# Strided q and k loaded as 108 rows, q/k weights loaded expert by expert, the last output tile in halves, and a new written-out order

## The chip, the cores and the metric

The kernel runs on one core of a Trainium2 chip. The metric is device time in microseconds (us), from one launch. Five engines each work through their own list of instructions in order: PE (TensorE, matrix products and transposes; its weight loads are shown as PEld), DVE (VectorE), ACT (ScalarE), POOL (GpSimd) and SP (SyncE, which here only issues DMA transfers). They wait for one another through semaphores.

## The reference

Inputs: q, k, v of shape (8 batches, 8 heads, 576 tokens, 64), and for each of 4 experts wq, wk, wv (512 x 64) and wo (64 x 512), plus a gate (512 x 4). First an attention with two kinds of sparse heads, then four dense causal attentions over its result, mixed by a top-2 gate:

```python
pos = np.arange(S); rel = pos[:, None] - pos[None, :]
mask_local = (rel >= 0) & (rel < 32)
mask_strided = (rel >= 0) & (pos[None, :] % 32 == pos[:, None] % 32)
# heads 0 to 3 local, heads 4 to 7 strided
x = softmax(where(mask, q @ k.T / 8, -1e9)) @ v      # to (8, 576, 512)
logits = x @ w_gate                                  # two largest of 4 experts, softmax over them
for e in range(4):
    a = softmax(causal((x @ wq[e]) @ (x @ wk[e]).T / 8))
    out += gate_weight(e) * (a @ (x @ wv[e]) @ wo[e])
```

A strided head attends among tokens whose positions agree modulo 32. With 576 tokens that is 32 groups of 18 tokens each.

## The kernel before, in words

**Stage 1** (`stage1(b, hp)`, head pair `hp` of batch `b`) computes the sparse attention of two heads: pairs 0 and 1 are local, 2 and 3 strided. q and k arrive in natural layout in a tile `nat`, are turned so that the 64 channels lie on partitions (tile `qkt`), scores go to PSUM (tiles `bank`), are masked into `p1l` (local) or `p1s` (strided), run through a softmax (maxima and sums on DVE, subtraction and scaling on POOL, the exponential on ACT), are turned back and multiplied with v (tile `v`); the result is written as two parts, `xh` and `xl`, whose sum is the value.

Batches 0 and 1 of the strided pairs turn q and k on PE (the loop at L595 to L609; from batch 2 on, `quad`, DVE does it). There the three residues of a strip of 11 groups lie in one tile: 54 rows of q on partitions 0 to 53, 54 rows of k on partitions 64 to 117, both heads side by side in the columns. Six DMAs bring q and k of such a head pair (L506, three strips each). Each transpose at L603 takes 54 rows by 128 columns, 24 of them per head pair; q's and k's alternate, and lie in different halves of the array's rows.

**Stage 2** (`project`, `values2`, `attend`, `out_tile`) projects x for two experts at a time (`ep` 0: experts 0 and 1; `ep` 1: experts 2 and 3), each product in three parts (L913, L925, L860), does the causal attention (L971, L1008, L1070, L1109) and the output product (L1138), copies the result from PSUM to a tile `ys` and stores it (L1147 to L1150). `load_weights` brings the q and k weights in four blocks of 128 input channels, all four experts in each block, and splits them into a rounded part (`wh`, ACT) and a rest (`wl`, DVE or POOL).

**The order.** The kernel's functions only record operations (`op`). `schedule()` issues them in the order of a table `ORDER`; a set `SECOND` says which operations take the second of two possible engines, and `FILL` says before which operations PE gets that many 128-column products of the identity with itself, whose result nobody reads (L304). So every engine's order follows from these tables. At the very start PE also gets five such products of ones (L1158).

PE's operations come in several tilings of its array (`mode`: "128x128" uses all rows and columns, "64x128" two halves of the rows, "64x64" quarters, and so on).

Of the kernel before, what the change touches and what calls it, by code (L numbers as in the profile page):

```python
# [8 lines left out]
F32 = mybir.dt.float32  # L9
# [11 lines left out]
def attention_moe_kernel(  # L21
# [59 lines left out]
    class Ring:  # L81
# [34 lines left out]
    }  # L116
    ORDER = [
# [1103 lines left out]
```

## Time and profile before

| | us |
|---|---|
| median of 3 runs (lowest to highest) | 440.24 (439.61 to 442.13) |
| the profiled execution, its own time | 439.54 |
| its span, first to last instruction | 437.8 |
| PE busy in it | 428.4 |
| DVE busy | 356.3 |
| ACT busy | 268.3 |
| POOL busy | 231.1 |

The profiled execution's time is 1.7 us more than its span and 0.7 us less than the median of the runs. PE's busy time counts the products that nobody reads too.

### The profile page before, as it was taken

Reading aid. Unit: us, or ns where it says so; the run is one execution under the profiler, and the core shown is the slowest. Engines: PE = TensorE matmul, PEld = TensorE weight load, DVE = VectorE, ACT = ScalarE, POOL = GpSimd, SP = SyncE. Lnnn points to the kernel's source line nnn. Section 1 sums busy time; section 2 is a strip of 40 time slices with the busy share of each in tenths; the row PEclk is TensorE's granted clock in tenths of the full one; section 3 lists DMA queues with packets and bytes.
Section 4 is the critical chain, followed back from the end, with each engine's and each line's share of the span. In section 5 each row is a group of like instructions: output and inputs, shape, how many; then the busy total and the mean of one; then the engine's idle time right before and its main releaser. Section 6 shows DMA issues by size and latency. Waiting matters only on the chain.

```text
span 437.8 us, 18842 instructions
## 1 busy us (share of the span) xinstructions
PE 428.4 (98%) x7588; PEld 376.6 (86%) x7588; DVE 356.3 (81%) x1140; ACT 268.3 (61%) x852; POOL 231.1 (53%) x375
## 2 busy tenths in 40 slices
PE   7999999999999999999999999999999999999996
PEld 6998998997789889788889788998789988998675
DVE  4798999899998896998889888896888888458750
ACT  4486647857676475566665378725577377557743
POOL 4164782678717842843819633679026771417720
PEclk9999999999999999999999999999999999999999
DMA  7665754766635634653256236355241030011113
GB/s 193 155 147 145 144 113 97 148 105 109 125 61 96 122 98 79 137 115 81 51 106 122 76 90 137 73 104 111 73 118 40 1 108 1 26 24 53 70 53 120
DMA packets 156271, 41.87 MB, mean 96 GB/s; under 512 B 145976, under 2 KB 149432, under 8 KB 156184
## 3 DMA queue, kind: packets, MB, share of 16 engines
q1 hardware_dynamic: 156184, 40.67, 42.0%
q8 instruction: 60, 0.98, 0.9%
q14 instruction: 27, 0.22, 0.2%
HBM read 31.20 MB, written 9.44 MB: 93 GB/s over the span
## 4 chain that ended last, share of the span: by engine, by line
PE 86%; DVE 5%; ACT 4%; DMA 2%; issue 1%; SPq 1%; POOL 1%; DVEq 0%; POOLq 0%; ACTq 0%
PE bank L913 19%; PE bank L1138 11%; PE bank L860 10%; PE bank L1109 10%; PE bank L1070 6%; PE bank L971 6%; PE bank L743 3%; PE bank L762 3%; PE bank L304 2%; PE bank L633 2%; PE bank L1008 2%; PE bank L649 2%; PE bank L713 2%; PE bank L925 2%; PE bank L823 1%
## 5 line engine op out<-in xcount | busy, mean ns | idle before, releaser
L1043 POOL TENSOR_SCALAR p<-p,st,wt 128x384 f32<-128x384 f32 (+3 forms) x128 | 77.3, 622 | 42.0 <-DVE st L1034 22.9
L983 ACT ACTIVATE p<-p,st 128x256 f32<-128x256 f32 (+3 forms) x128 | 72.1, 568 | 9.1 <-DVE st L978 8.9
L978 DVE CUSTOM_DVE_ANT_0 p<-bank,m_cau 128x128 f32<-128x128 f32 (+3 forms) x128 | 57.5, 481 | 3.1 <-PE bank L971 2.9
L526 DVE STREAM_TRANSPOSE qkt<-nat 128x576 f32<-128x576 f32 x48 | 47.7, 1004 | 3.5 <-DMA nat<-in_k_dram 3.1
L1109 PE MATMUL bank<-th,vs 128*64 128x192 f32 (+4 forms) x512 | 49.2, 338 | 0.0
L341 ACT COPY th<-bank 128x256 f32<-128x256 f32 (+2 forms) x104 | 40.6, 431 | 12.2 <-PE bank L1070 11.7
L676 POOL TENSOR_TENSOR p1l<-p1l,st 128x640 f32<-128x640 f32 (+1 forms) x18 | 20.7, 1154 | 49.6 <-DVE st L674 40.0
L1109 PEld LDWEIGHTS bank<-th,vs 128*64 128x64 f32 x512 | 34.1, 137 | 14.2 <-issue 7.0
L934 ACT CAST qk<-bank 128x288 fp32r<-128x288 f32 x64 | 25.0, 399 | 30.6 <-PE bank L913 22.8
L725 ACT CAST xh<-bank 128x160 fp32r<-128x160 f32 (+4 forms) x112 | 28.9, 321 | 22.4 <-PE bank L743 9.9
L727 DVE TENSOR_TENSOR xl<-bank,xh 128x160 fp32r<-128x160 f32 (+4 forms) x112 | 31.6, 323 | 6.4 <-ACT xh L725 5.7
L860 PE MATMUL bank<-wh_v,xh 128*128 128x260 f32 x128 | 36.5, 285 | 0.3 <-DVE qkl L936 0.3
L913 PE MATMUL bank<-xh,wh_k 128*128 128x288 f32 x120 | 36.5, 304 | 0.2 <-DVE st L978 0.2
L860 PE MATMUL bank<-wh_v,xl 128*128 128x260 f32 x128 | 36.2, 283 | 0.0
L913 PE MATMUL bank<-xh,wh_q 128*128 128x288 f32 x120 | 36.2, 302 | 0.0
L860 PE MATMUL bank<-wl_v,xh 128*128 128x260 f32 x128 | 36.1, 282 | 0.0
L1070 PEld LDWEIGHTS bank<-ident,p 64*128 64x128 f32 x800 | 30.5, 139 | 6.5 <-issue 3.0
L1070 PE MATMUL bank<-ident,p 64*128 64x64 f32 x800 | 35.2, 227 | 0.5 <-DVE pt L341 0.5
L913 PE MATMUL bank<-xl,wh_q 128*128 128x288 f32 x120 | 35.4, 295 | 0.0
L913 PE MATMUL bank<-xl,wh_k 128*128 128x288 f32 x120 | 35.4, 295 | 0.0
L913 PE MATMUL bank<-xh,wl_k 128*128 128x288 f32 x120 | 35.3, 294 | 0.0
L913 PE MATMUL bank<-xh,wl_q 128*128 128x288 f32 x120 | 35.3, 294 | 0.0
(188 smaller groups left out, 1268.0 us busy)
## 6 DMA issues: line engine op xcount, KB each, us to landing
out_dram<-ys SPq DMA_DIRECT2D x32, 256.0 KB
nat<-in_q_dram SPq DMA_DIRECT2D x96, 72.0 KB
nat<-in_k_dram SPq DMA_DIRECT2D x96, 72.0 KB
v<-in_v_dram SPq DMA_DIRECT2D x96, 40.0 KB
v<-in_v_dram SPq DMA_DIRECT2D x48, 54.0 KB
v<-in_v_dram SPq DMA_DIRECT2D x32, 48.0 KB
v<-in_v_dram SPq DMA_DIRECT2D x32, 45.0 KB
out_dram<-ys SPq DMA_DIRECT2D x8, 128.0 KB
```

Of the source, the lines that this page charges most:

```text
L341: (nc.scalar.copy if e == "ACT" else nc.vector.tensor_copy)(dst, src)
L526: op("tq", {"DVE": 0.66 if local else 1.11}, k0 - 13, lambda e, x=x: nc.vector.transpose(turned(qkt.t, x), raw(x) if local else raw(x).rea ...
L725: op("xh", {"ACT": act(n_) + 0.04 * (not local)}, key, lambda e, s_=s_, x_=x_: nc.scalar.copy(x_(xh.t), s_(xa.t)), r=[xa], w=[xh[u]])
L727: op("xl", {"DVE": dve(n_)}, key + 0.5, lambda e, s_=s_, x_=x_: nc.vector.tensor_sub(x_(xl.t), s_(xa.t), x_(f(xh.t))), r=[xa, xh[u]], w=[x ...
L860: nc.tensor.matmul(vp.t[:, :NV], xx.t[:, t0:t0 + 128], ww.t[:, kt, :], start=i == 0, stop=i == 11)
L913: nc.tensor.matmul(pj.t[:, :HS], ww.t[:, kt, ep * 128:(ep + 1) * 128], xx.t[:, c], start=i == 0, stop=i == 11)
L978: lambda e, sp=sp, p=p, a=a, nk=nk, ci=ci, st=st[ep]: nc.vector.tensor_tensor_reduce(out=p.t[:, a, :nk], in0=sp[a].t[:, :nk], in1=m_cau[:, ...
L983: op("exp2", {"ACT": 0.285 + 0.00084 * nk}, k_ + 1, lambda e, p=p, a=a, ci=ci, nk=nk, st=st[ep]: nc.scalar.activation(p.t[:, a, :nk], p.t[ ...
L1043: lambda e, p=p, a=a, ci=ci, t=t, nk=nk, s_=s_, ep=ep: nc.gpsimd.tensor_scalar(p.t[:, a, :nk], p.t[:, a, :nk], s_.t[:, 20 + ci + a:21 + ci ...
L1070: nc.tensor.transpose(tp[hf].t[:, 64 * c:64 * c + 64], src, ident[r, r])
L1109: nc.tensor.matmul(acc.t[o, c0:c0 + cn], vw, th[ep, a].t[:, s0:s0 + cn], start=j == 0, stop=j == nj - 1, skip_group_check=True)
L1138: nc.tensor.matmul(yp.t[:, :DM], xx.t[:, c0:c0 + 128], ww.t[:, ep, :], start=i == 0, stop=i == 5)
```

## The change

Seven things change. The recorded operations are partly others, so the tables `ORDER`, `SECOND` and `FILL` are new throughout.

1. Strided q and k of batches 0 and 1: one DMA each for q and for k of a head pair, 108 rows (2 heads x 18 x 3 strips) of 11 x 64 elements, instead of three DMAs of 18 partitions and two pieces each. A third strip then has an eleventh group too, which is the next row's first and is masked or not used.
2. The transposes of these take 108 rows by 128 columns, 12 per head pair instead of 24, in the full-array tiling.
3. The order of tokens in a group of 54 is another (position, then strip), so these scores get a mask of their own, `m_tri`, made at the start; v of these pairs is loaded in the same order.
4. wq and wk are loaded and split expert by expert; projections of experts 0 and 1 wait for the weights of these two only.
5. Batch 7's tile 3, the last one stored, is computed, copied and stored in two halves of 256 columns.
6. `FILL` holds 36 products in place of 61.
7. The new `ORDER` and `SECOND`.

```diff
-        8: 5, 13: 6, 18: 7, 51: 1, 56: 3, 76: 1, 89: 4, 92: 5, 96: 1, 124: 4, 131: 2, 148: 4, 208: 2, 218: 1,
-        241: 2, 246: 8, 279: 2, 282: 3, 1132: 2, 1150: 3, 1151: 4,
+        3: 1, 13: 2, 51: 3, 61: 4, 76: 1, 93: 4, 95: 4, 126: 1, 130: 2, 135: 4, 217: 1, 245: 2, 260: 1, 285: 4,
+        292: 2, 1146: 3, 1151: 1, 1157: 8, 1158: 2, 1160: 3,
...
+    m_tri = const.tile([128, 54], F32, name="m_tri")
+    m_res = const.tile([128, 3, NJ + 1], F32, name="m_res")
+    nc.vector.memset(m_res, NEG)
+    for hf in range(2):
+        v_ = m_res[64 * hf:64 * hf + 64, :, :NJ]
+        nc.gpsimd.affine_select(out=v_, in_=v_, pattern=[[-1, 3], [-3, NJ]], compare_op=ALU.not_equal,
+                                fill=0.0, base=0, channel_multiplier=1)
+    nc.vector.tensor_reduce(m_res[:, :, NJ], m_res[:, :, :NJ], axis=mybir.AxisListType.X, op=ALU.max)
+    nc.vector.tensor_copy(m_tri.rearrange("p (u r) -> p u r", r=3), m_res[:, :, NJ].unsqueeze(1).to_broadcast([128, NJ, 3]))
+    for hf in range(2):
+        keep(m_tri[64 * hf:64 * hf + 64], [[-1, 54]], 0, 1)
...
+        if name in "qk":
+            for ex in range(E):
...
+                op("load_0", {"SP": 0.5}, k_ + 0.1 * ex, lambda e, ex=ex, raw=raw: nc.sync.dma_start(
+                    raw(), src[ex].rearrange("(a p) d -> p a d", p=128)), w=[st], dmas=[(0.47, 0.71)])
...
-                for r in range(3):
-                    n_ = (11 if r < 2 else 10) * D
-                    p_ = 64 * x + NJ * r
-                    nc.sync.dma_start(nat.t[p_:p_ + NJ, :22 * D].rearrange("p (h c) -> p h c", h=2)[:, :, :n_], strips(base, 11 * r, n_))
+                nc.sync.dma_start(nat.t[:6 * NJ, 12 * D * x:12 * D * x + 11 * D], triples(base, 0, 2 * NJ, 11))
...
+        def triples(base, g0, m, gn):
+
+            return bass.AP(tensor=base.tensor, offset=base.offset + g0 * D, ap=[[STR * D, m], [11 * D, 3], [1, gn * D]])
...
-                for g in range(6):
-                    for x in range(2):
-                        r = slice(64 * x, 64 * x + 54)
-                        c = (11 * u + 2 * g) * D
-                        nc.tensor.transpose(tp[x].t[:, 54 * g:54 * g + 54], nat.t[r, c:c + 128], ident[r, r])
+                    r = slice(0, 6 * NJ)
+                    for g in range(3):
+                        c = (12 * x + 6 * u + 2 * g) * D
+                        nc.tensor.transpose(tp.t[:, 108 * g:108 * g + 108], nat.t[r, c:c + 128], ident[r, r])
...
     def wbufs(nm, ep=0):
-        return [W[nm][i][kt, ep] for i in range(2) for kt in range({"o": E * D // 128}.get(nm, KT))]
+        parts = range(2 * ep, 2 * ep + 2) if nm in "qk" else range(E * D // 128 if nm == "o" else KT)
+        return [W[nm][i][x] for i in range(2) for x in parts]
...
+        cut = 2 if b == B - 1 and t == 3 else 1
+        n_ = DM // cut
+        for h in range(cut):
...
+                        nc.tensor.matmul(yp.t[:, :n_], xx.t[:, c0:c0 + 128], ww.t[:, ep, c], start=i == 0, stop=i == 5)
...
+                    nc.sync.dma_start(out[b, t0:t0 + 128, c], ys.t[:, c])
```

Where the new tables move instructions, three places show it. The first is SP's list at the start of the program, before the change: `p` and `nat` are the tiles for q and k of stage 1, and a name in brackets is the semaphore waited for; DMAHW0 to DMAHW7 are those of earlier transfers in turn.

```order
L501 DMA p_169<-in_q_dram 128x576
L501 DMA p_169<-in_k_dram 128x576
L501 DMA p_170<-in_q_dram 128x576
L501 DMA p_170<-in_k_dram 128x576
L506 DMA nat_179<-in_q_dram 18x2x704 [waits DVE_49]
L506 DMA nat_179<-in_q_dram 18x2x640
L506 DMA nat_179<-in_k_dram 18x2x704 [waits DMAHW0_49]
L506 DMA nat_179<-in_k_dram 18x2x640 [waits DMAHW1_49]
L501 DMA nat_183<-in_k_dram 128x576 [waits DMAHW2_49,DVE_49]
L427 DMA p_167<-in_moe_w_gate_dram 128x2x4 [waits DMAHW3_49]
L501 DMA nat_183<-in_q_dram 128x576 [waits DMAHW4_49]
```

The same place of SP's list after the change:

```order
L528 DMA p_182<-in_k_dram 128x576
L528 DMA p_182<-in_q_dram 128x576
L530 DMA nat_192<-in_k_dram 108x1x704
L528 DMA p_183<-in_k_dram 128x576
L528 DMA p_183<-in_q_dram 128x576
L530 DMA nat_192<-in_q_dram 108x1x704
L438 DMA p_180<-in_moe_w_gate_dram 128x2x4
L530 DMA nat_195<-in_k_dram 108x1x704
L580 DMA v_205<-in_v_dram 32x5x64 [waits DMAHW0_49]
```

The first strided pair's k stood in the eighth to tenth place and stands in the third; its q stood in the fifth to seventh and stands in the sixth; all of q and k of batch 0's four head pairs but one q is issued before the first transfer that has to wait for an earlier one.

The second place is PE's list behind the five products of ones, before the change: L304 are the products nobody reads, L574 and L587 transposes of local pairs, L603 those of strided pairs, L633 local scores (the alternating rows of one score operation are cut to two).

```order
L304 MATMUL bank1_65<-ident_83 128x128 x5
L574 MATMUL bank1_65<-ident_83,p230_169 128x128 x4
L574 MATMUL bank2_66<-ident_83,p230_169 128x128 x4
L304 MATMUL bank3_67<-ident_83 128x128 x6
L587 MATMUL bank3_67<-ident_83,p230_169 128x128 x2
L574 MATMUL bank4_68<-ident_83,p231_170 128x128 x4
L304 MATMUL bank5_69<-ident_83 128x128 x7
L633 MATMUL bank5_69<-qkt0_191 32x64
L633 MATMUL bank6_70<-qkt0_191 32x64
```

The same place after the change; L305 are the products nobody reads, L608 and L621 the local transposes, L637 the strided ones.

```order
L305 MATMUL bank1_65<-ident_83 128x128
L608 MATMUL bank1_65<-ident_83,p230_182 128x128 x4
L608 MATMUL bank2_66<-ident_83,p230_182 128x128 x4
L305 MATMUL bank3_67<-ident_83 128x128 x2
L621 MATMUL bank3_67<-ident_83,p230_182 128x128 x2
L305 MATMUL bank4_68<-ident_83 128x128 x4
L637 MATMUL bank4_68<-ident_83,nat0_192 128x108 x3
L305 MATMUL bank5_69<-ident_83 128x128 x4
L637 MATMUL bank5_69<-ident_83,nat0_192 128x108 x3
L665 MATMUL bank6_70<-qkt0_201 32x64
L665 MATMUL bank7_71<-qkt0_201 32x64
```

Ahead of the first local scores there stood 18 unread products and stand 11; six strided transposes now come before these scores.

The third place is the end of PE's list, the last output tile, after the change (before it there were six rows of 128x512 into one bank).

```order
L1176 MATMUL bank7_71<-wh_o0_280,oh2_266 128x256
L1176 MATMUL bank7_71<-wh_o0_280,ol2_269 128x256
L1176 MATMUL bank7_71<-wl_o0_281,oh2_266 128x256
L1176 MATMUL bank7_71<-wh_o0_280,oh0_264 128x256
L1176 MATMUL bank7_71<-wh_o0_280,ol0_267 128x256
L1176 MATMUL bank7_71<-wl_o0_281,oh0_264 128x256
L1176 MATMUL bank6_70<-wh_o0_280,oh2_266 128x256
L1176 MATMUL bank6_70<-wh_o0_280,ol2_269 128x256
L1176 MATMUL bank6_70<-wl_o0_281,oh2_266 128x256
L1176 MATMUL bank6_70<-wh_o0_280,oh0_264 128x256
L1176 MATMUL bank6_70<-wh_o0_280,ol0_267 128x256
L1176 MATMUL bank6_70<-wl_o0_281,oh0_264 128x256
```

The first half's six products go to bank 7, the second half's six to bank 6; the copy of bank 7 stands on DVE, that of bank 6 on ACT.

Counted over PE's whole list, changes from one tiling of the array to another fall from 197 to 183.

## Rows read from the trace of the kernel before

**Rows 1.** The page: PE's busy time, and the chain by engine.
```profile
PE 428.4 (98%) x7588; PEld 376.6 (86%) x7588; DVE 356.3 (81%) x1140; ACT 268.3 (61%) x852; POOL 231.1 (53%) x375
PE 86%; DVE 5%; ACT 4%; DMA 2%; issue 1%; SPq 1%; POOL 1%; DVEq 0%; POOLq 0%; ACTq 0%
```

**Rows 2.** Waits of PE, 42 to 438 us: total us, times, longest us.
```profile
PE bank L762 <- issue: 0.8, 1, 0.8
...
PE bank L1008 <- POOL p L996: 0.2, 1, 0.2
```

**Rows 3.** Timeline of PE, the start: start us, us, instruction, shape, count.
```profile
7.00 1.77 PE L304 MATMUL bank<-ident 128*128 128x128 f32 x10
8.61 1.04 PE L574 MATMUL bank<-ident,p 128*128 128x128 f32 x8
9.48 1.50 PE L304 MATMUL bank<-ident 128*128 128x128 f32 x12
10.82 0.38 PE L587 MATMUL bank<-ident,p 128*128 128x128 f32 x2
...
16.89 0.58 PE L603 MATMUL bank<-ident,nat 54*128 54x54 f32 x12
17.41 1.16 PE L304 MATMUL bank<-ident 128*128 128x128 f32 x8
...
22.77 0.95 PE L603 MATMUL bank<-ident,nat 54*128 54x54 f32 x24
23.65 0.71 PE L304 MATMUL bank<-ident 128*128 128x128 f32 x4
...
27.00 1.11 PE L743 MATMUL bank<-pt,v 32*64 32x32 f32 x84
...
42.38 0.40 PE L925 MATMUL bank<-xh,wh_k 128*128 128x288 f32 x1
```

**Rows 4.** Timeline of PE behind a change of tiling.
```profile
45.11 0.40 PE L925 MATMUL bank<-xh,wh_k 128*128 128x288 f32 x1
45.35 0.30 PE L925 MATMUL bank<-xl,wh_k 128*128 128x288 f32 x1
45.48 0.29 PE L925 MATMUL bank<-xh,wl_k 128*128 128x288 f32 x1
```

**Rows 5.** Timeline of SP's DMA issues, the start.
```profile
4.00 1.06 SPq L506 DMA_DIRECT2D nat<-in_k_dram  x3
6.24 0.36 SPq L501 DMA_DIRECT2D nat<-in_k_dram  x1
...
12.46 1.42 SPq L506 DMA_DIRECT2D nat<-in_k_dram  x3
```

**Rows 6.** Timelines of DVE and POOL, their first work on loaded data; idle before in brackets.
```profile
9.75 1.19 DVE L341 COPY qkt<-bank 64x256 f32<-64x256 f32 x3 [4.37 <-PE bank L574]
...
16.04 1.41 POOL L676 TENSOR_TENSOR p1l<-p1l,st 128x320 f32<-128x320 f32 x2 [9.56 <-ACT qkt L341]
```

**Rows 7.** Windows of DVE: stretch, us, busy (count), granted TensorE clock, DMA share, GB/s.
```profile
0.00:20.00 20.00, 11.50 (x63) 1.00 0.65 166
20.00:120.00 100.00, 94.25 (x279) 1.00 0.63 128
120.00:438.00 318.00, 250.57 (x801) 1.00 0.36 81
```

**Rows 8.** Timeline of the end, all engines.
```profile
433.68 0.39 PE L1138 MATMUL bank<-wl_o,oh 128*128 128x512 f32 x1
...
434.11 0.59 ACT L341 COPY ys<-bank 128x512 f32<-128x512 f32 x1 [0.73 <-PE bank L1138]
434.72 0.44 SPq L1150 DMA_DIRECT2D out_dram<-ys  x1
```

**Rows 9.** Groups by line and shape: ACT's copies of 256 columns (busy, mean ns | idle).
```profile
L341 ACT COPY th<-bank 128x256 f32<-128x256 f32 x44 | 15.8, 378 | 5.7 <-PE bank L1070 5.5
```

More of the change, by code (lines that the diff above doesn't have):

```diff
@@ L418, in load_weights @@
         hi, lo = W[name]
-        eps = (0, 1) if name in "qk" else (0,)
         k_ = first("w" + name)
@@ L430, in load_weights, with raw @@
                w=[wide[i][0], wide[i][1]], dmas=[(0.5, 0.2)])
+        if name in "qk":
+            for ex in range(E):
+                st = wide[ex // 2][ex % 2]
+                def raw(ex=ex):
+                    return flat(ex // 2)[:, ex % 2 * n:ex % 2 * n + n].rearrange("p (a d) -> p a d", d=D)
+                c = slice(ex * D, ex * D + D)
+                op("load_0", {"SP": 0.5}, k_ + 0.1 * ex, lambda e, ex=ex, raw=raw: nc.sync.dma_start(
+                    raw(), src[ex].rearrange("(a p) d -> p a d", p=128)), w=[st], dmas=[(0.47, 0.71)])
+                op("hi_w", {"ACT": 0.1 + act(n)}, 15 + k_ * 0.1, lambda e, c=c, raw=raw: nc.scalar.copy(hi.t[:, :, c], raw()),
+                   r=[st], w=[hi[ex]])
+                op("lo_w", {"DVE": 0.1 + dve(n), "POOL": 0.1 + 0.0025 * n}, 15.5 + k_ * 0.1, lambda e, c=c, raw=raw: (
+                    nc.vector if e == "DVE" else nc.gpsimd).tensor_sub(lo.t[:, :, c], raw(), f(hi.t[:, :, c])),
+                   r=[st, hi[ex]], w=[lo[ex]])
+            return
         for kt in range(nk):
@@ L445, in load_weights @@
             op("hi_w", {"ACT": 0.1 + act(n)}, 15 + k_ * 0.1, lambda e, kt=kt, raw=raw: nc.scalar.copy(hi.t[:, kt, :], raw()),
-               r=[st], w=[hi[kt, ep] for ep in eps])
+               r=[st], w=[hi[kt]])
             op("lo_w", {"DVE": 0.1 + dve(n), "POOL": 0.1 + 0.0025 * n}, 15.5 + k_ * 0.1, lambda e, kt=kt, raw=raw: (
                 nc.vector if e == "DVE" else nc.gpsimd).tensor_sub(lo.t[:, kt, :], raw(), f(hi.t[:, kt, :])),
-               r=[st] + [hi[kt, ep] for ep in eps], w=[lo[kt, ep] for ep in eps])
-    NAT = fixed("nat", [128, (11 * 2 + 1) * D], 3, value=lambda t: [t[:, c * D:(c + 1) * D] for c in (10, 21, 22)])
+               r=[st, hi[kt]], w=[lo[kt]])
+    NAT = fixed("nat", [128, 24 * D], 3, value=lambda t: [t[:, c * D:(c + 1) * D] for c in (11, 23)])
     QKT = fixed("qkt", [128, 4 * 6 * 54], 2, value=lambda t: [t[:, 2 * S:2 * S + NJ]])
@@ L486, in qg @@
         def qg(x, h, g, cn):
-            c = ((2 * x + h) * 6 + g // 2) * 54
+            c = (12 * x + 2 * (g // 2) + h) * 54
             return qkt.t[64 * (g % 2):64 * (g % 2) + 64, c:c + cn]
@@ L502, in load_qk @@
             else:
-                for r in range(3):
-                    n_ = (11 if r < 2 else 10) * D
-                    p_ = 64 * x + NJ * r
-                    nc.sync.dma_start(nat.t[p_:p_ + NJ, :22 * D].rearrange("p (h c) -> p h c", h=2)[:, :, :n_], strips(base, 11 * r, n_))
+                nc.sync.dma_start(nat.t[:6 * NJ, 12 * D * x:12 * D * x + 11 * D], triples(base, 0, 2 * NJ, 11))
         def strips(base, g0, n_):
             return bass.AP(tensor=base.tensor, offset=base.offset + g0 * D, ap=[[STR * D, NJ], [S * D, 2], [1, n_]])
-        dm = [(0.51, 0.48)] if quad else [(0.44, 1.15)] if local else [(0.34, 0.67)] * 3
+        def triples(base, g0, m, gn):
+            return bass.AP(tensor=base.tensor, offset=base.offset + g0 * D, ap=[[STR * D, m], [11 * D, 3], [1, gn * D]])
+        dm = [(0.51, 0.48)] if quad else [(0.44, 1.15)] if local else [(0.5, 1.5)]
         for x, src in enumerate((q, k)):
@@ L514, in stage1 @@
                 op(*(("load_qk", {"SP": 0.54}, k0 - 30) if b > 1 else ("load_0", {"SP": 0.54}, first("x", b, hp))),
-                   lambda e, src=src, x=x, h=h, y=y: load_qk(src, x, h, y), w=[nat[x]] if quad else [nat], dmas=dm)
+                   lambda e, src=src, x=x, h=h, y=y: load_qk(src, x, h, y), w=[nat] if local and not quad else [nat[x]], dmas=dm)
         def turned(t, x):
@@ L552, in load_v @@
                     dma.dma_start(vv()[32 * j:32 * j + 32, m0:, h, :], ap)
+            elif not quad:
+                for r in range(3):
+                    for x, (g0, g1) in enumerate(((0, 6), (6, 11))):
+                        n_ = (g1 - g0) * D
+                        dma.dma_start(vt.t[64 * x + r:64 * x + 54:3, :2 * 6 * D].rearrange("p (h c) -> p h c", h=2)[:, :, :n_],
+                                      strips(base, 11 * r + g0, n_))
             else:
@@ L594, in stage1, with tps @@
                    r=[tp], w=[qkt[0], qkt[1]])
-        for u in range(0 if quad or local else 2):
-            tp = [RB.new(f"tp{u}{x}_{n}") for x in "qk"]
-            def tps(e, tp=tp, u=u):
-                for g in range(6):
-                    for x in range(2):
-                        r = slice(64 * x, 64 * x + 54)
-                        c = (11 * u + 2 * g) * D
-                        nc.tensor.transpose(tp[x].t[:, 54 * g:54 * g + 54], nat.t[r, c:c + 128], ident[r, r])
-            op("tp", {"PE": 0.063 * 6}, k0 - 14 + u, tps, r=[nat], w=[*tp, qkt[0], qkt[1]], mode=MR)
-            for x in range(2):
-                c0 = (2 * x + u) * 324
-                op("tp_out", either(324), k0 - 13 + u, lambda e, t_=tp[x], c0=c0: copy(
-                    e, qkt.t[:, c0:c0 + 324], t_.t[:, :324]), r=[tp[x]], w=[qkt[0], qkt[1]])
+        for x in range(0 if quad or local else 2):
+            for u in range(2):
+                tp = RB.new(f"tp{u}{x}_{n}")
+                def tps(e, tp=tp, x=x, u=u):
+                    r = slice(0, 6 * NJ)
+                    for g in range(3):
+                        c = (12 * x + 6 * u + 2 * g) * D
+                        nc.tensor.transpose(tp.t[:, 108 * g:108 * g + 108], nat.t[r, c:c + 128], ident[r, r])
+                op("tp", {"PE": 0.115 * 3}, k0 - 14 + 0.5 * x + 0.2 * u, tps, r=[nat[x]], w=[tp, qkt[x]], mode=M128)
+                op("tp_out", either(324), k0 - 13 + 0.5 * x + 0.2 * u, lambda e, tp=tp, c=648 * x + 324 * u: copy(
+                    e, qkt.t[:, c:c + 324], tp.t[:, :324]), r=[tp], w=[qkt[x]])
         for h in range(2 if local else 1):
@@ L652, in stage1 @@
         N = 2 * ni * nk
-        msk = m_loc if local else m_str.unsqueeze(1).to_broadcast([128, 6, 54])
+        msk = m_loc if local else (m_str if quad else m_tri).unsqueeze(1).to_broadcast([128, 6, 54])
         def pv():
@@ L757, in values1 @@
                             continue
-                        n_ = 54 if g < 10 else 36
+                        n_ = 54 if g < 10 or not quad else 36
                         m, b_ = divmod(s_, 2)
@@ L769, in cols @@
                     c = 54 * (g0 % 6)
-                    return t[:, c:c + 54 * gn].rearrange("c (g r u) -> c u r g", r=3, u=NJ)[:, :, :rn]
+                    return t[:, c:c + 54 * gn].rearrange("c (g r u) -> c u r g" if quad else "c (g u r) -> c u r g", r=3, u=NJ)[:, :, :rn]
                 def toks(t):
@@ L928, in project @@
                     op("pj", {"PE": 3 * 0.132}, key + step * u + 0.1 * kt, part,
-                       r=[X[b, kt][i][x] for i in range(2) for x in range(4)] + [W[nm][i][kt, 0] for i in range(2)],
+                       r=[X[b, kt][i][x] for i in range(2) for x in range(4)] + wbufs(nm),
                        w=[pj, qk[j, u]], mode=M128)
@@ L1129, in out_tile, with mm, store @@
         c0 = 0 if last else QT[t][0]
-        yp, ys = RB.new(f"yp_{b}_{t}"), YS.new(f"ys_{b}_{t}")
+        ys = YS.new(f"ys_{b}_{t}")
         src = [OF[b // 2, ep] if last else O[b, ep] for ep in range(2)]
         need = [x[i] for pair in src for x in pair for i in ((0, 1) if last else (int(t > 2),))]
-        def mm(e):
-            i = 0
-            for ep in range(2):
-                for xx, ww in split3(src[ep], W["o"]):
-                    nc.tensor.matmul(yp.t[:, :DM], xx.t[:, c0:c0 + 128], ww.t[:, ep, :], start=i == 0, stop=i == 5)
-                    i += 1
-        op("yp", {"PE": 6 * 0.229}, key, mm, r=need + wbufs("o"), w=[yp, ys], mode=M128)
-        op("yp_out", either(DM), key + 0.5, lambda e: copy(e, ys.t, yp.t[:, :DM]), r=[yp], w=[ys])
-        def store(e):
-            t0 = QT[t][0]
-            if last:
-                nc.sync.dma_start(out[b - 1, t0:, :], ys.t[:64, :])
-                nc.sync.dma_start(out[b, t0:, :], ys.t[64:, :])
-            else:
-                nc.sync.dma_start(out[b, t0:t0 + 128, :], ys.t)
-        op("store", {"SP": 0.5}, key + 1, store, r=[ys], dmas=[(0.4, 0.4)] * 2 if last else [(0.4, 0.8)])
+        cut = 2 if b == B - 1 and t == 3 else 1
+        n_ = DM // cut
+        for h in range(cut):
+            yp = RB.new(f"yp_{b}_{t}" + "b" * h)
+            c = slice(h * n_, (h + 1) * n_)
+            def mm(e, yp=yp, c=c):
+                i = 0
+                for ep in range(2):
+                    for xx, ww in split3(src[ep], W["o"]):
+                        nc.tensor.matmul(yp.t[:, :n_], xx.t[:, c0:c0 + 128], ww.t[:, ep, c], start=i == 0, stop=i == 5)
+                        i += 1
+            op("yp", {"PE": 6 * 0.229 / cut}, key + h, mm, r=need + wbufs("o"), w=[yp, ys[h]], mode=M128)
+            op("yp_out", either(n_), key + h + 0.5, lambda e, yp=yp, c=c: copy(e, ys.t[:, c], yp.t[:, :n_]), r=[yp], w=[ys[h]])
+            def store(e, c=c):
+                t0 = QT[t][0]
+                if last:
+                    nc.sync.dma_start(out[b - 1, t0:, :], ys.t[:64, :])
+                    nc.sync.dma_start(out[b, t0:, :], ys.t[64:, :])
+                else:
+                    nc.sync.dma_start(out[b, t0:t0 + 128, c], ys.t[:, c])
+            op("store", {"SP": 0.5}, key + h + 1, store, r=[ys[h]], dmas=[(0.4, 0.4)] * 2 if last else [(0.4, 0.8)])
     wb = RB.new("warm")
```

303 rows, old and new, of tables (ORDER, SECOND) are left out of this document.

## The prediction

> **What bounds the kernel now.** I read the page's busy times first: PE is busy 428.4 of 437.8 us, and the chain that ends last lies on PE for 86% [rows 1]. So PE's list is the length of the kernel, and the question is what that list holds. The waits of PE come next: from 42 us to the end there are seven, of 0.8 to 0.2 us, 3.0 us in all [rows 2]. Third, the timeline of PE's start, because a busy PE need not be a useful one. Up to the first projection (L925) at 42.38 us it is filled with products that nobody reads, L304 [rows 3]: the table FILL asks for 61. One of them is two records: the five in front of the first transposes stand there as x10. Twelve records from 9.48 to 10.82 take 1.34 us, so 0.112 a record and 0.224 a product; 61 of them are 13.7 us. Before about 8 us PE is slower: the ten records from 7.00 to 8.61 take 1.61 us, 0.5 more than later ones [rows 3]. DVE is the second engine to look at. It has 8.5 us free in the first 20 us, but only 5.8 of the next 100 [rows 7]. Where PE gets its work earlier, DVE has to follow.
>
> **The change, part by part.** The sum is made against the profiled execution, 439.54 us.
>
> *Fewer unread products.* 25 fewer, 25 x 0.224 = **5.6 us less** on PE. This holds if what they covered is no longer waited for. What is covered is in the first place the wait for loads and for the chain of copies and softmax behind them. For the loads: SP's list shows that each transfer waits for the eighth before it, and SP's issues show when these landed. The third transfer, a 128-row load of 295 KB, lets the eleventh go at 6.24; the strided pair's last piece, the tenth, lets the eighteenth go at 12.46 [rows 5]. So the first strided pair was whole at about 12.5 us. In the new list its k is third and its q sixth; with them 0.9 and 1.8 MB have been moved. The third transfer had 0.88 MB moved by 6.24, so k is there at about 6.3 us; at the 166 GB/s of the first 20 us [rows 7] the further 0.9 MB take 5.4 us, so q is there by 11.7 at the latest, by 9.0 at twice that rate. PE wants the first of the two behind 7 unread products and ten local transposes: 7.00 + 0.5 (the slow start) + 7 x 0.224 + 10 x 0.109 = 10.2 us, and the other four products and three transposes later, at 11.4. So the first has 4 us of room, the second between none and 2.4. For the chain: PE reaches the first value products (L743), which need the whole softmax of the first pair, behind 28 unread products where it had 42; those come at 27.00 now [rows 3] and would come 14 x 0.224 = 3.1 us earlier less what moves in front of them. The first scores come 7 x 0.224 = 1.6 us earlier, less six transposes of 0.1, 1.0 us. So the softmax has to give up about 2 us of what it had. DVE has that room here: it sits idle 4.37 us before its first copy of loaded data, and POOL 9.56 before its first subtraction [rows 6].
>
> *Transposes.* The old 96 come in six groups: start to next start 0.52 us for twelve (16.89 to 17.41) and 0.88 for 24 (22.77 to 23.65) [rows 3]; the four of twelve and two of 24 add to 3.75 us. The new 48 have no row. From below: they are like L574 (128 rows by 128 columns, eight from 8.61 to 9.48, 0.109 each), with 108 of 128 columns to stream, 0.092. From above: 0.109. Between them, a straight line from the old form (54 streamed columns, 0.073 for each of the two halves of the rows) to L574 gives 0.10; I take that, 4.8 us, **1.05 us more** (0.7 to 1.5). The Trainium skill, page "TensorE: Matmul & The Clock Gate", section "LDWEIGHTS (loading the stationary operand)", says that a weight load takes its number of columns divided by 1.2 ns whatever the rows, 107 ns for the 128 here; by that 48 take 5.1 us and the sum is 0.3 us worse. The old transposes do not bear it out as a floor: their loads have 128 columns too, and one per half of the rows takes 0.073 [rows 3].
>
> *Changes of tiling.* A change costs 0.1 us on the step behind it (45.11 to 45.35, 0.24 where the next step is 0.13) [rows 4] and, as an estimate, up to as much on the step ahead. There are 14 fewer. Eleven belong to the old groups of transposes, whose way out is in the 3.75 already; five ways in at 0.1 and three others at 0.1 make **0.8 us less** (0 to 2.8, if none or all 14 count, at 0.2).
>
> *Loads.* Six DMAs of a pair become two; 16 issues fewer on SP, by about 0.35 us each (three in 1.06 [rows 5]) 5.6 us of SP's time in the first 35 us. SP is not in the chain, so I count nothing; it lies behind PE's work, and it is what brings the loads forward above. The weights by expert are the same eight transfers and splits of the same size; nothing. v of these pairs moves in the same six pieces each; nothing.
>
> *The mask.* Four selections on POOL and three short operations on DVE, all before 8 us. POOL then has 9.56 us free and DVE 4.37 [rows 6]; nothing. Without that cover it would be about 2 us.
>
> *The last tile in halves.* Now the last product starts at 433.68, its copy of 512 columns takes 0.59 us from 434.11, the store is issued at 434.72 [rows 8] and the span ends at 437.8, 3.1 us later. The last copy will have 256 columns, 0.38 us [rows 9]: 0.2 less. The first half's copy and issue (0.38 + 0.44) run beside the second half's 0.7 us of products. Half the bytes in the last store save between nothing and 1 us of the 3.1; I take 0.2. Together **0.4 us less** (0.2 to 1.2).
>
> *The order behind 42 us.* The same products in another sequence. PE's waits there are 3.0 us now [rows 2]; the new order has others, which no row tells. Bounds: none (3 us gained) and twice as many (3 us lost); I take the same number, **0**.
>
> Sum: -5.6 + 1.05 - 0.8 - 0.4 = -5.75, so a profiled execution of 433.8 us. The median of the runs stands 0.7 us above the profiled execution; **434.5 us**, 1.3% faster than the median of 440.24.
>
> **The rivals.** *DVE holds PE back.* From 20 to 120 us DVE is busy 94.2 of 100 us [rows 7]. To have PE 5 us earlier by 120 us, DVE must be earlier as well. It can start 1.2 us sooner (the first transposes move from 8.61 to about 7.4) and leave out the idle pieces it now has while loads come, some 2 us; past that it would have to run at 99% instead of 94%. If it can't, the gain is these 3.2 us and the 0.4 of the tail: 436.6 us. For it speaks how full that row is; against it, that from 120 us on DVE is busy for 79% only [rows 7], so what lags may be made good there.
>
> *The unread products become waits.* They may cover something that the change does not bring forward: in this case PE stands idle for 5.6 us and only the rest of the sum is left, -0.15: 440 us, no change. For it: the chain between 23 and 37 us runs through copies and softmax and not through loads; there PE filled its time. Against it: 14 of the 25 dropped products stood in front of the first value products, where loads landed late.
>
> *Slower: the clock of TensorE does not rise or falls back.* PE ran slowly until about 8 us and then at twice the pace [rows 3], with a granted clock that reads 1.00 (2.4 GHz) in every stretch of the view [rows 7]. In the new start it gets 28 unread products up to the first value products where it had 42, and transposes in their place. If these did not hold the clock up, each us of PE's work would take one more. From 5.7 us of such work on nothing is gained, from 7.9 on it is slower by over 0.5%, and if it lasts from 8 us to the first value products at about 23 us it costs 15: 449.5 us. Against it: eight transposes in a row stood in the old list too, from 8.61, and the twelve records behind them ran at 0.112 [rows 3]. The Trainium skill, same page, section "Part 4: PE-mode transpose", says that transposes do not count as work that raises the clock; by that this rival is the likelier one at the very start, where eight transposes now come after one unread product. No run here shows a start with transposes alone.
>
> **How the numbers follow.** Forecast as summed: 0.55, with its own range of 432 to 437 (the transposes' -0.35 to +0.45, the tilings' -2.0 to +0.8, the tail's -0.8 to +0.2, waits of -3 to +3, of which I let half go each way at once). DVE holds back: 0.20, 436.6. Products become waits: 0.17, 440. Clock: 0.08, 449.5. Within 0.5%, 2.2 us, which is about what a measurement of this kernel can tell from no change, lie 438.04 to 442.44. Faster takes the forecast, DVE's case and a little of the third: 0.76; no change the rest of the third and an upper tail of the order's waits: 0.16; slower 0.08. The range: 431.8 to 439.2 leaves out the clock, half of the case of waits and a lower tail of some 0.04, together 0.2.
>
> **What would show it.** In the profile after: L637 (the new transposes) first at about 10 us and 48 of them at 0.10 each; 72 records of the unread products instead of 122; the first value products at 23 to 25 us and the first projection between 28 and 34; PE's waits behind 42 us near 3 us; the last store issued 0.6 us after the last product's end instead of 1.0. Wrong it would be if PE showed waits of over 3 us in the first 60 us (loads or DVE), if DVE's busy share from 20 to 120 us reached 98%, or if steps of 128-column records stayed at 0.21 past 9 us.

## The result, and the profile after

The changed kernel takes 445.37 us (median of 12 runs, 443.96 to 447.5), the kernel before beside it 440.56 (12 runs, 439.2 to 444.04). The ratio is 1.0103, with a 95% interval of 1.0076 to 1.013: **1.0% slower**, 4.8 us, where 434.5 and 1.3% faster had been forecast. The profiled execution took 445.06 us.

The page of the changed kernel, PE's busy time and the chain by engine (against [rows 1]):

```profile
PE 428.1 (97%) x7496; PEld 373.6 (84%) x7496; DVE 361.0 (81%) x1135; ACT 270.2 (61%) x862; POOL 230.4 (52%) x375
...
PE 76%; SPq 8%; DVE 6%; DMA 4%; issue 2%; ACT 1%; POOL 1%; DVEq 0%; ACTq 0%
```

PE's busy time is the same to 0.3 us; the span is 5.5 us longer. SP's issues hold 8% of the chain, where they held 1% [rows 1], and loads 4% instead of 2%. That points to SP and what it loads. PE's waits from 42 us on (total us, times, longest us; against [rows 2]):

```profile
PE bank L794 <- DMA v<-in_v_dram: 3.5, 2, 3.1
PE bank L1176 <- DVE xl L759: 0.7, 1, 0.7
```

Two waits, of 3.1 us and then 0.4, are longer than all of PE's waits there before together. They are for v of the second of batch 1's two strided pairs in PE's list. The timeline of PE around it:

```profile
68.91 0.69 PE L1041 MATMUL bank<-p,qw 64*64 64x288 f32 x7
72.71 0.32 PE L794 MATMUL bank<-pt,v 54*64 54x54 f32 x4 [3.11 <-DMA v<-in_v_dram]
73.44 1.33 PE L794 MATMUL bank<-pt,v 54*64 54x54 f32 x40 [0.41 <-DMA v<-in_v_dram]
74.50 1.26 PE L1041 MATMUL bank<-p,qw 64*64 64x288 f32 x8
```

Seven products of one form take 0.69 us ahead of the wait, eight take 1.26 behind it: the clock has fallen to its lower level, 1.2 GHz. The windows of PE show it as a granted clock of 0.91 over that stretch (us, busy, granted clock, DMA share, GB/s):

```profile
60.00:80.00 20.00, 15.84 (x407) 0.91 0.55 106
80.00:100.00 20.00, 20.00 (x340) 1.00 0.66 117
```

Why v is late is read on SP. Its issues of v of the strided pairs of batches 0 and 1, before the change:

```profile
29.77 2.11 SPq L558 DMA_DIRECT2D v<-in_v_dram  x6
...
35.91 2.34 SPq L558 DMA_DIRECT2D v<-in_v_dram  x6
...
58.95 2.20 SPq L558 DMA_DIRECT2D v<-in_v_dram  x6
...
67.74 2.10 SPq L558 DMA_DIRECT2D v<-in_v_dram  x6
```

and after it, with a q load of 108 rows in the first line:

```profile
23.09 0.81 SPq L530 DMA_DIRECT2D nat<-in_q_dram  x1
...
25.61 4.98 SPq L585 DMA_DIRECT2D v<-in_v_dram  x6
...
32.13 5.24 SPq L585 DMA_DIRECT2D v<-in_v_dram  x6
...
61.65 9.91 SPq L585 DMA_DIRECT2D v<-in_v_dram  x12
```

Six issues take 5 us where they took 2.2, 0.83 each instead of 0.37. The number of transfers and their bytes are nearly the same; what differs is that their 18 partitions stand three apart (`vt.t[64 * x + r:64 * x + 54:3]`), so that v has the new token order. From 25.61 to 71.56 us SP issues one transfer behind the other, with a single pause of over 0.15 us (0.45 at 47.0); it reaches the twelve issues for batch 1 at 61.65 and is done with them at 71.56. The end of the chain that leads to the wait for v (start us, us, what):

```profile
69.99 0.76 SPq L585
...
70.80 2.52 DMA v<-in_v_dram
...
73.44 1.33 PE bank L794 x40
```

The start itself went much as forecast: the new transposes begin at 10.45, the first value products at 24.10, the first projection at 33.21 (42.38 before, [rows 3]):

```profile
10.45 0.44 PE L637 MATMUL bank<-ident,nat 108*128 108x108 f32 x3
10.73 1.07 PE L305 MATMUL bank<-ident 128*128 128x128 f32 x8
...
24.10 0.34 PE L775 MATMUL bank<-pt,v 32*64 32x32 f32 x12
...
33.21 0.38 PE L958 MATMUL bank<-xh,wh_k 128*128 128x288 f32 x1
```

### The profile page after: what moved, and what is told of

Same layout as the page of the kernel before. It is cut to its first block, busy times and chain, and to the rows that moved or that the text cites. A ratio compares the mean times of both kernels' runs of the same rounds, so it can differ in the third digit from the quotient of the medians.

```text
span 443.3 us, 18610 instructions
## 1 busy us (share of the span) xinstructions
PE 428.1 (97%) x7496; PEld 373.6 (84%) x7496; DVE 361.0 (81%) x1135; ACT 270.2 (61%) x862; POOL 230.4 (52%) x375
## 4 chain that ended last, share of the span: by engine, by line
PE 76%; SPq 8%; DVE 6%; DMA 4%; issue 2%; ACT 1%; POOL 1%; DVEq 0%; ACTq 0%
PE bank L946 19%; PE bank L1176 11%; PE bank L1142 9%; PE bank L893 8%; PE bank L1103 6%; PE bank L1004 5%; PE bank L775 3%; SPq L525 3%; PE bank L665 3%; SPq L580 3%; PE bank L681 2%; DMA v<-in_v_dram 2%; PE bank L1041 2%; DVE qkt L554 2%; PE bank L856 1%
## 5 line engine op out<-in xcount | busy, mean ns | idle before, releaser
L1011 DVE CUSTOM_DVE_ANT_0 p<-bank,m_cau 128x256 f32<-128x256 f32 (+3 forms) x128 | 58.2, 481 | 2.5 <-PE bank L1004 1.7
L342 ACT COPY th<-bank 128x384 f32<-128x384 f32 (+2 forms) x101 | 39.9, 434 | 14.4 <-PE bank L1103 13.7
L759 DVE TENSOR_TENSOR xl<-bank,xh 128x128 fp32r<-128x128 f32 (+4 forms) x112 | 32.8, 323 | 9.7 <-ACT xh L757 9.3
```

Of the source, the lines that this page charges most:

```text
L342: (nc.scalar.copy if e == "ACT" else nc.vector.tensor_copy)(dst, src)
L759: op("xl", {"DVE": dve(n_)}, key + 0.5, lambda e, s_=s_, x_=x_: nc.vector.tensor_sub(x_(xl.t), s_(xa.t), x_(f(xh.t))), r=[xa, xh[u]], w=[x ...
L1011: lambda e, sp=sp, p=p, a=a, nk=nk, ci=ci, st=st[ep]: nc.vector.tensor_tensor_reduce(out=p.t[:, a, :nk], in0=sp[a].t[:, :nk], in1=m_cau[:, ...
```

## The experiments

Theory A: the issues with partitions three apart put SP behind, v of batch 1 lands late, PE waits 3.5 us, and its clock falls. Theory B: the new order waits anyway, for DVE or elsewhere. Theory C: the fewer unread products and the transposes let the clock fall. Each ratio is to the kernel before on the same chip. Where v's rows or values are exchanged, no amount of work changes.

**e1: v in four transfers of 54 adjacent partitions.**

```diff
-                for r in range(3):
-                    for x, (g0, g1) in enumerate(((0, 6), (6, 11))):
-                        n_ = (g1 - g0) * D
-                        dma.dma_start(vt.t[64 * x + r:64 * x + 54:3, ...], strips(base, 11 * r + g0, n_))
+                for x, (g0, g1) in enumerate(((0, 6), (6, 11))):
+                    for y in range(2):
+                        dma.dma_start(vt.t[64 * x:64 * x + 54, 6 * D * y:6 * D * y + (g1 - g0) * D],
+                                      triples(v[b, h0 + y], g0, NJ, g1 - g0))
```

> The changed kernel, but v of the strided pairs of batches 0 and 1 goes in four transfers of 54 adjacent partitions (one for each head and half) in place of six whose 18 partitions stand three apart. Theory A (the spaced issues put SP behind, so v of batch 1 lands late, PE waits 3.5 us at 69 us and its clock then falls): an issue takes about 0.45 us by rows of 0.33 for 36 pieces and 0.81 for 108, a pair under 2 us instead of 5; the waits for v at 69 us are gone, the clock stays up, the time falls by 4 to 7 us from 445.4 to 438 to 441. Theory B (the new order itself waits, for DVE or elsewhere): the wait for v only gives way to another and the time stays at 444 to 446. Theory C (fewer unread products and full-array transposes let the clock fall): the half-clock stretch at 73 us stays and the time falls by 3.5 us at most.

438.0 us (10 runs), ratio 0.9947 (0.9922 to 0.9972). The wait for v at 69 us is gone and 7 us are back, as A says. B and C, which expected 444 us or 442 and above, are out as the main cause. One number of A was wrong: an issue still takes 0.76 us, though its partitions are adjacent. A pair takes 3.3 us because it has four issues instead of six:

```profile
27.44 3.36 SPq L584 DMA_DIRECT2D v<-in_v_dram  x4
...
61.29 6.70 SPq L584 DMA_DIRECT2D v<-in_v_dram  x8
```

**e2: six transfers of 18 adjacent partitions.** The rows of v then don't match the scores' order.

```diff
-                        dma.dma_start(vt.t[64 * x + r:64 * x + 54:3, ...], strips(base, 11 * r + g0, n_))
+                        dma.dma_start(vt.t[64 * x + NJ * r:64 * x + NJ * r + NJ, ...], strips(base, 11 * r + g0, n_))
```

> The changed kernel, but the six transfers of v of the strided pairs of batches 0 and 1 go to 18 adjacent partitions each, as before the change, in place of partitions three apart. Number, bytes and sources of the transfers are the same; v then stands in another row order than the scores, so the output of these pairs is another one. Theory A (the spacing of the partitions is what costs): an issue falls from 0.83 to about 0.33 us, the wait for v at 69 us goes, 438 to 441 us, the same as with 54 adjacent partitions. Rival (the issue's length comes from where SP stands, for example from a full queue, and not from the spacing): issues stay near 0.8 us and the time at 445.

438.5 us (10 runs), ratio 0.9937 (0.9912 to 0.9961), and six issues in 2.2 us again. Only the step between the partitions was changed, so the step is the cause:

```profile
26.02 2.23 SPq L585 DMA_DIRECT2D v<-in_v_dram  x6
```

**e3: the kernel before with v three partitions apart.**

```diff
-                        dma.dma_start(vt.t[p_:p_ + NJ, ...], strips(base, 11 * r + g0, n_))
+                        dma.dma_start(vt.t[slice(64 * x + r, 64 * x + 54, 3) if b < 2 else slice(p_, p_ + NJ), ...], strips(base, 11 * r + g0, n_))
```

> The kernel before, with one thing of the change: its 24 transfers of v of the strided pairs of batches 0 and 1 go to partitions three apart; the row order then doesn't match the scores, so the output of these pairs is another one. Theory A: issues go from 0.33 to 0.8 us, 11 us more of SP's time, by 60 us; v of batch 1 was issued there at 59 us and needed after 70, so 5.5 us of delay for the second half of the issues may just be hidden: 440.5 to 444 us. If the spaced issue is cheap in the old order (rival: it is slow only in the new order): 440 us with issues of 0.33.

448.02 us (4 runs), ratio 1.0181 (1.0137 to 1.0226): the step alone makes the old kernel 1.8% slower, more than the upper end A gave. The issues are the long ones here too, so they don't come from the new order. PE waits 2.3 us for v in its profile, and the clock falls twice, at 44.7 and 75.4 us, for 3.4 us each:

```profile
30.41 5.11 SPq L558 DMA_DIRECT2D v<-in_v_dram  x6
```

**e4 and e8: unread products in the place of the wait.** The changed kernel with `304: 14` added to `FILL`.

> The changed kernel with 14 unread products (about 3.1 us) in PE's list ahead of the first value products of batch 1's first strided pair, that is in the place of its wait for v at 69 us. The data is as late as before. Theory A with two parts (a wait of 3.5 us, and then 3.4 us of half clock that the wait brought on): the stretch at half clock goes and 1.5 to 2.8 us come back, 442.5 to 444 us. If the clock falls for another reason: no gain, 445 us.

> The kernel of e4 again (the changed kernel with 14 unread products in the place of the wait for v), since e4's profile was of a disturbed execution; its timed runs gave 446.6, no gain. If covering the wait holds the clock up, the profile shows 1.00 from 60 to 80 us, and then what the 2 us went to instead: products that run on behind the arrival of v. If the clock falls in spite of them, the profile shows a stretch at half speed behind 70 us.

e4 took 444.9 to 447.6 us in four runs (ratio 1.0125, 1.0081 to 1.0168), e8's one execution 445.43: no gain, where A had forecast 442.5 to 444. e8's timeline of PE:

```profile
70.69 3.39 PE L305 MATMUL bank<-ident 128*128 128x128 f32 x28
74.01 0.32 PE L794 MATMUL bank<-pt,v 54*64 54x54 f32 x4
74.53 0.80 PE L794 MATMUL bank<-pt,v 54*64 54x54 f32 x40 [0.20 <-DMA v<-in_v_dram]
75.13 0.70 PE L1041 MATMUL bank<-p,qw 64*64 64x288 f32 x8
```

The eight products behind the wait take 0.70 us, so the clock stayed up in this execution. But the last of v landed at 74.40 us, where it had landed at 73.31 in the changed kernel: two of SP's issues for it took 1.6 and 1.4 us instead of 0.8. The next projections then start at 77.31, against 77.47. So the delay of v took most of what the clock gave back, and the filling itself ran until 74.01, beyond the 72.71 at which PE had gone on in the changed kernel. This one execution speaks for the wait having brought the clock down and against theory C. What a shorter filling would have gained, and why v came later, it does not show.

**e7 and e11: 54 partitions from evenly spaced rows.** As e1, but the rows of v are others (step 640 elements):

```diff
-                                      triples(v[b, h0 + y], g0, NJ, g1 - g0))
+                                      bass.AP(tensor=vb.tensor, offset=vb.offset + g0 * D, ap=[[10 * D, 54], [1, (g1 - g0) * D]]))
```

> The kernel of e1, whose issues of 54 partitions took 0.76 us although their partitions are adjacent, with one thing changed: the rows of the source stand at one even step (640 elements) instead of 18 times three strips, so v holds other values and the output of these pairs is another one. If the issue is long because 54 partitions are written, it stays at 0.76 us. If it is long because the transfer's partitions come in two nested steps (18 times 3), as the 18 partitions three apart also do, it falls to 0.3 us, and the time is within 1 us of e1's timed runs, 437 to 439.

> The kernel of e7 again, timed: v of the strided pairs in four transfers of 54 adjacent partitions from evenly spaced rows (other values of v, so the output of these pairs is another one), issues of 0.28 us, 1.2 us of SP for a pair where e9 takes 2. If SP is still what the start waits for, 1 to 2 us faster than e9; if not, the same as e9 within 1 us.

```profile
25.52 1.48 SPq L585 DMA_DIRECT2D v<-in_v_dram  x4
```

Four issues in 1.5 us (e7) instead of 3.3 (e1), with the same number of rows of the same length. So with 54 adjacent partitions the issue is long where the rows of the source come in two nested steps (18 times 3). The 18 partitions three apart have a single step on either side and are long all the same; what the two forms share is not shown. Timed (e11), this gives 438.83 us (10 runs), 0.9955 (0.9929 to 0.998), no better than e1: at 3.3 us for a pair (e1) and below, SP no longer sets the time. e7's one execution, 435.96, lies below all ten of e11's (437.49 to 441.11).

**e9: 18 adjacent partitions, and the mask step writes its columns in that order.** This does the whole computation.

```diff
-                pv()[:, h], sp[h].t[:, :ni * nk].rearrange("p (i c) -> p i c", c=nk), msk, ALU.add),
+                pu(pv()[:, h]), us(sp[h].t[:, :ni * nk].rearrange("p (i c) -> p i c", c=nk)), us(msk), ALU.add),
```

`us` reads the 54 columns as (u r), `pu` writes them as (r u), for these pairs alone.

> The changed kernel with v of the strided pairs of batches 0 and 1 in six transfers of 18 adjacent partitions, strip by strip, as in e2, and the mask step writing its columns in that order, so that the scores match and the whole computation is done. Theory A: issues of 0.3 us, no wait for v at 69 us, clock up; 436.5 to 438.5 us, as e2, 0.5 to 0.9% faster than before. If the reordered columns cost DVE time on each of 8 mask steps (16 instructions of 54 x 6 elements, at worst twice their 0.4 us), DVE is 6 us later by 70 us and PE waits for it: 440 or more.

438.71 us (12 runs), 0.9952 (0.992 to 0.9985): faster than before and than the changed kernel, the same as e1. The mask step did become dearer, 768 ns where it was 480 (groups by line and shape), but there are eight such instructions and not sixteen, 2.3 us of DVE in all (the changed kernel's line, then e9's):

```profile
L695 DVE TENSOR_TENSOR p1s<-bank,m_tri 128x324 f32<-128x324 f32 x8 | 3.7, 480 | 0.1
...
L701 DVE TENSOR_TENSOR p1s<-bank,m_tri 128x324 f32<-128x324 f32 x8 | 5.8, 768 | 0.1
```

The other runs measure the largest term of the forecast, the unread products.

**e5: e1 without the 36 products; e6: the kernel before without its 61** (`FILL = {}`).

> The kernel of e1 (v in transfers of 54 partitions) without the 36 unread products of the table FILL; the five products of ones at the start stay. If an unread product costs its whole 0.224 us, as the prediction's largest term had it, the time falls by 8.1 us from 438 to 430. If they stand where PE would wait anyway, little changes: 437 to 439. If they hold the clock up, it rises: 440 to 446, and the profile shows records of half speed after 9 us.

> The kernel before without its 61 unread products. By the prediction's price for each (0.224 us) the time falls by 13.7 us from 440.5 to 427. By the rival they fill waits: 438 to 441 with waits of PE of about 10 us in the first 40 us. If they hold the clock up: 442 to 450 and records of half speed after 8 us.

e5: 439.88 us, 1.0007 (0.9979 to 1.0036), against e1's 0.9947: 0.6% slower without them. e6: 441.02 us, 1.0015 (0.9997 to 1.0034). 61 products that take 13.7 us of PE bring nothing when they go. e6's windows of PE and its longest waits before 45 us show what stands in their place:

```profile
10.00:20.00 10.00, 7.08 (x241) 0.83 0.71 170
20.00:30.00 10.00, 7.21 (x229) 0.83 0.61 152
30.00:40.00 10.00, 8.37 (x271) 0.65 0.67 168
```

```profile
PE bank L630 <- ACT qkt L338: 4.4, 2, 2.8
...
PE bank L630 <- DVE xl L724: 1.4, 1, 1.4
```

PE waits for the copies out of PSUM and runs at the lower clock for part of the time between.

**e10: e9 with 60 products.** 24 more, at seven of the places that had some.

```diff
-        3: 1, 13: 2, 51: 3, 61: 4, 76: 1, 93: 4, 95: 4, 126: 1, 130: 2, 135: 4,
+        3: 5, 13: 6, 51: 5, 61: 8, 76: 1, 93: 8, 95: 4, 126: 1, 130: 4, 135: 8,
```

> The kernel of e9 with 60 unread products instead of 36, the 24 more at places in PE's list up to 26 us where such products stand already. By the prediction's price (0.224 us for each) the time rises by 5.4 us above e9. By the runs without any (e5 and e6: no gain) the products mostly stand where PE would wait: up to 2 us slower.

445.61 us (4 runs), 1.0116 (1.0058 to 1.0175): 6.9 us above e9, 0.29 us for each. Not all of this is the products' own time: its profile has a wait of PE that e9's has not, and behind it 3.4 us at the lower clock.

```profile
PE bank L662 <- issue: 2.2, 1, 2.2
```

**e12: the kernel before with 36 products.**

```diff
-        8: 5, 13: 6, 18: 7, 51: 1, 56: 3, 76: 1, 89: 4, 92: 5, 96: 1, 124: 4, 131: 2, 148: 4, 208: 2, 218: 1,
-        241: 2, 246: 8, 279: 2, 282: 3, 1132: 2, 1150: 3, 1151: 4,
+        8: 1, 13: 2, 18: 8, 51: 1, 56: 3, 76: 1, 89: 2, 92: 3, 96: 1, 124: 3, 131: 1, 148: 3, 208: 1, 218: 1,
+        241: 1, 246: 3, 282: 1}
```

> The kernel before with 36 unread products in place of 61, 11 of them ahead of the first local scores as in the changed kernel, the rest thinned out; nothing else is changed. By the prediction's term (25 fewer at 0.224 us) the time falls by 5.6 us from 440.5 to 435. By the rival that they fill waits, and by e6 (none of them: no gain), it stays within 1 us of before, and the profile shows waits and slow steps of PE of about 5 us more in the first 45 us.

446.27 us (6 runs), 1.0131 (1.0096 to 1.0166). The term of -5.6 us, tried alone, is **+6**. Neither the forecast nor its rival had that. The profile is of its slowest execution (448.44). Behind 7 us PE waits 9.2 us in it, 6.0 of them of the kind called issue, against 2.9 and 0.8 before, and the clock is down for 17 us in three stretches; the other five runs have a granted clock of 0.985 to 0.992, so it fell in all of them. Its longest waits of PE in the first 100 us, and a piece of its timeline:

```profile
PE bank L630 <- issue: 2.3, 1, 2.3
PE bank L740 <- issue: 2.0, 1, 2.0
```

```profile
62.25 1.09 PE L740 MATMUL bank<-pt,v 32*64 32x32 f32 x77
65.37 0.43 PE L740 MATMUL bank<-pt,v 32*64 32x32 f32 x7 [2.02 <-issue]
...
70.15 0.42 PE L857 MATMUL bank<-wl_v,xh 128*128 128x260 f32 x1
70.36 0.42 PE L857 MATMUL bank<-wh_v,xh 128*128 128x260 f32 x1
```

PE stops 2 us in the middle of a group of 84 small products, waiting for nothing that the profile shows, and then runs at the lower clock until about 71.7: a step of L857 is 0.21 us at 70.15, and 0.12 once the clock is up again.

## Why the prediction was wrong

**Loads: the step that failed.** "v of these pairs moves in the same six pieces each; nothing", and "SP is not in the chain, so I count nothing". The pieces were the same, but not the way they are written. 24 issues at 0.83 us instead of 0.37 are 11 us more of SP's time. And the fewer q and k loads, counted as 5.6 us less of SP, saved 0.6: the 24 issues took 7.2 us, the eight of 108 rows 6.7. SP got into the chain (8%), v came late, PE waited 3.5 us for it and its clock fell behind that wait. Taking this alone out of the changed kernel gives back about 7 us (e1, e2, e9, e11: 438.0 to 438.8), putting it alone into the old one costs 8 (e3). Of the 10.6 us between the forecast change (-5.75) and the measured one (+4.8), some 7 are this; the rest lies in the terms below. The signs that the prediction named for being wrong missed it: they end at 60 us, and the wait comes at 69. The trace of before had the price of a plain issue only, but the prediction named no bound for another form. A row of the trace could have been one: three strips in 1.06 us [rows 5] are 0.35 each for 36 rows, and nothing showed that the new forms, 108 rows or partitions three apart, cost the same. A sum with 0.35 to 1 us an issue would have put this term between nothing and 16 us of SP.

The Trainium skill, page "Perfetto Trace Analysis", section "What 'DMA-bound' means", says that where the issuing engine's track is solid, what is seen is the generation of descriptors, and that larger descriptors are the remedy. The trace agrees with the first as far as it shows: SP issues from 25.61 to 71.56 with one pause of over 0.15 us. No run has larger descriptors; but e1 and e7 move as many rows of the same length, in 0.8 and 0.4 us an issue, the pause behind it included, so the length of the rows is not what sets these two apart.

**The unread products: a term of the wrong price.** "25 x 0.224 = 5.6 us less" rested on the remark that this holds if what they covered is no longer waited for, and that was looked into for the first loads, scores and softmax only. In the old kernel 25 fewer cost 6 us (e12), 61 fewer nothing (e6); in the new one 36 fewer cost 2 to 2.6 (e5 against e1, by medians and by ratios), 24 more cost 6.9 (e10). So no single price per product holds here: in e6 a product taken out became a wait for copies, in e12 most of the new waits are for nothing that the profile shows, and the clock fell behind them. The rival "the unread products become waits" was right in kind. This is why the changed kernel with v mended stands at -2.0 to -2.8 us and not at -5.75: as sums of PE's steps (start to next start, from the two traces), e9 has 5.9 us less of unread products and 1.75 less at changes of tiling, but 2.3 us more of waits and 0.7 more of transposes; some 3 us more lie in slower steps between them, which no run took apart.

**The clock.** The rival had its place wrong. At the start it rose about as before, at 8.6 us against 8.0: the eight transposes at 7.43 took 0.18 us each, those of before 0.109 [rows 3], some 0.6 us lost. It fell at 73.5 us instead, behind the wait for v, and stayed down for 3.4 us, some 1.7 us of PE's work lost. The profiled execution shows little of this: its mean granted clock is 0.995, that of the twelve timed runs 0.987 to 0.996, and that of the kernel before in the runs beside the experiments 0.996 to 1.000. So most runs were at the lower level for longer than the profile shows.

**DVE.** Its busy time from 20 to 120 us is 88.7 of 100 us, lower than before [rows 7], but there PE's waits for v held DVE up too. In e9, where they are all but gone (0.4 us), it is 94.7, the same as before, and PE's waits for DVE behind 42 us are 3.0 us, none over 0.7, against 1.5 before. So waits for DVE cost 1.5 us more there; whether a freer DVE would give more was not tried.

**The order behind 42 us.** Without the two for v, PE's waits there are 3.7 us against 2.9, inside the bounds.

**The small terms.** PE waits nowhere for the new mask; the last of its selections on POOL ends at 7.45 us. Transposes: the three from 10.45 to 10.73 took 0.093 each; 48 at that are 4.5 us, +0.7 and not +1.05, the lower bound. The Trainium skill, page "TensorE: Matmul & The Clock Gate", section "LDWEIGHTS (loading the stationary operand)", puts the load of 128 columns at 0.107, as an estimate of the step; the trace is below it, with 0.093. Tilings: -1.6 to -1.75 as sums of the steps behind a change alone, inside the range. The tail was not worth 0.4: from the start of the last product to the end of the span it is 4.25 us (439.05 to 443.3) against 4.1 before [rows 8], because the store of the last half waits on SP behind two other stores:

```profile
439.05 0.28 PE L1176 MATMUL bank<-wl_o,oh 128*128 128x256 f32 x1
439.12 0.59 SPq L1186 DMA_DIRECT2D out_dram<-ys  x1
439.41 0.37 ACT L342 COPY ys<-bank 128x256 f32<-128x256 f32 x1 [0.84 <-PE bank L1176]
439.80 1.03 SPq L1188 DMA_DIRECT2D out_dram<-ys  x2
```

## What to carry to other kernels

An engine that only issues transfers is a resource with a price per issue, and the price depends on how the partitions and the rows of the source are walked: look it up in the trace for the very form that the change makes, and if no row has it, put both bounds into the sum, even where the engine is off the chain today. Work that nobody reads is not a gain waiting to be taken: first see what PE would wait for in its place, and what its clock does behind that wait. Where a layout must change, let a step that walks memory freely (a mask, a copy) take the permutation, and keep the transfer plain, or make fewer transfers of it.

## What the runs showed of the hardware

- An issue of v of a strided pair held SP for 0.27 to 0.38 us in nearly all cases where it went to 18 adjacent partitions (before, e2, e9), and as nearly always for 0.76 to 0.84 where these stood three apart (after, e3). To 54 adjacent partitions it took 0.75 to 0.83 from rows in two nested steps (18 times 3, e1) and 0.27 to 0.38 from evenly spaced rows (e7); 108 rows (36 times 3) took 0.78 to 1.0. The other loads of these kernels mostly took 0.3 to 0.53, single ones up to 2 us.
- PE's waits that the profile calls "issue" go with the loading of its instructions. Eleven of the traces have such waits of over 0.25 us, 20 in all and up to 2.75 us long; all lie in or next to groups of small products, and each of them ended 1.2 to 1.7 us after a 16 KB transfer of the queue "instruction" had landed. Four of them, from the trace:

```
kernel              wait us   ends at   block landed   after us
e12_before_36          2.30     36.41          34.86       1.55
e12_before_36          2.02     65.37          63.90       1.47
e5_v54_nofill          2.75     33.12          31.77       1.34
e10_v18_morefill       2.17     38.00          36.74       1.26
```

  That PE ran out of instructions there is read from these times, not tried; what sets the times of the blocks stays open.
- The clock fell in or right behind a wait of 3.1 us (after), of 2.0 (e12) and of 1.4 (e1's profiled execution, its slowest with 440.7), and not behind one of 1.1 (e2). But it also fell within 1.4 us behind one of 0.8 (e3, at 43.4) and within 0.2 behind one of 0.7 (e11, at 207.7), and behind one of 1.4 at 28.8 in e6 it stayed up for 4 us more. So the length of one wait does not tell. In the cases where it fell it stayed down for 3 to 7 us, on a PE that was busy again.
- The same mask addition took 480 ns with columns in order and 768 with the 54 columns written in another order (e9).
